# Retention and a bilinear FFN on one core: how the first pairs of slots keep their state and form their outputs

## The chip, the cores and the metric

The kernel runs on one core of one Trainium2 chip. The metric is the time of one execution in device microseconds, as the median of several runs. Beside it stands one profiled execution, from which every view of the trace comes.

## The reference

The work is a retention layer and, behind it, a feed-forward network (FFN) without a bias.

```python
batch, n_heads, seq, head_dim = (4, 8, 768, 64)
gamma = 1.0 - 2.0 ** (-5.0 - np.arange(H))
for t in range(S):
    state = gamma * state + einsum('bhd,bhe->bhde', k[:, :, t], v[:, :, t])
    y[:, :, t] = scale * einsum('bhd,bhde->bhe', q[:, :, t], state)
x = y.transpose(0, 2, 1, 3).reshape(B * S, H * D)        # 3072 x 512
out = ((x @ w_a) * (x @ w_b)) @ w_out                    # d_ff 1536
```

The inputs and the output are float32. The kernel computes with bfloat16 operands and float32 sums.

## The kernel before, in words

The 3072 rows of x are 24 *slots* of 128 rows, six to each of the four batches. The FFN works on blocks of 2 or 4 slots (`TILES`). For each block and each of 12 slices of d_ff (`ft`), `ffn_a` forms a = x w_a and ScalarE (ACT) copies it to SBUF (`asb`); `ffn_g` forms g = x w_b and VectorE (DVE) multiplies the two into `ht`; `ffn_out` multiplies by w_out. These products are L504, L516 and L544.

The decay of the state is put into k and q: both are multiplied by tables of powers of gamma (`scaled`, L212), so that the state is a plain sum of products of k and v. Inside a chunk of 128 positions, the output is the masked product of q and k, times v; what lies before the chunk comes from q times the state.

The first batch's six slots are done as three *pairs* (u = 0, 1, 2), with even positions in one slot of the pair and odd ones in the other. A pair has two chunks c = 0 and c = 1. The functions of a pair are:

- `casts2`: the scaling of k and q (L212) and the cast of v to bfloat16 (L184), each on a given engine. GpSimd (POOL) scales pair 1's k and one slot of its q; DVE scales pair 0 and the other slot of pair 1's q.
- `flip2`: transposes of scaled k or q on TensorE (PE, L395) into a bank of PSUM, and a copy to SBUF (`kT`, `qT`; L182 on ACT, L184 on DVE).
- `scores2`: 16 products of k and q (L408) for one slot of the pair, into two banks (`at`); `mask2`: two DVE products with a mask (L418), which give `aT`.
- `update2`: 16 products of k and v (L431) added to the state, which stays in one bank of PSUM (`st`). `keep_state` then copies the state to SBUF for use as an operand.
- `intra2`: 16 products of v and `aT` (L460) into the two banks `ys[u][0]` and `ys[u][1]`, one for each chunk; `inter2`: products of the state and q (L448) on top of these.
- `leave2`: the *exit*: each bank of y is copied to `xt`, the FFN's operand, on a given engine (L182 or L184).
- `warm`: products of zeros (L483), whose results nobody reads.

In the kernel before, the state of two halves of the heads (r = 0 and 1, 64 partitions each) is copied by `keep_state` as two blocks into a block-diagonal tile of 128 rows (`gbd`), with zeros elsewhere. `inter2` then has a contraction of 128 rows: 8 products for pair 0, which has no state ahead of its first chunk, and 16 for each later pair.

PSUM has eight banks: three under the tag `ff`, handed round among `flip2`, `scores2` with `ff=True` and the FFN's a, g and o; two under `at`; one each under `y0` and `y1`; one under `st`. A tile that takes over a bank waits until the last reader of the one before is done.

The order on each engine is the order in which the program is written: the helper `seq` ties each instruction to the one before it on its engine. Waits between engines follow from the tiles that instructions write and read. So the order of the calls at the end of the function is the schedule. The last of the calls that matter here are `ffn_a(0, 0, 0, W2)` and `ffn_a(0, 1, 0, W2)`, a(0,0) and a(0,1) for the first 256 columns (pair 0), then `ffn_g(0, 0, 0, W2)`, and then `ffn_a(0, 0, W2, 2 * W2)`, the same slice for the 256 columns of pair 1; in the timeline it opens a group of eight products of L504.

`fenced` and `into` are used by later batches already: a marker copy on ACT or DVE that waits for PE's last product, and a dependency by which the next products into the same banks wait for the marker ("rows change banks").

Of the kernel before, what the change touches and what calls it, by code (L numbers as in the profile page):

```python
# [9 lines left out]
F32 = mybir.dt.float32  # L10
# [6 lines left out]
PAIRS = 3  # L17
# [6 lines left out]
def kernel(  # L24
# [10 lines left out]
    nc = tc.nc  # L35
    P = 128
    B, H, S, D = q.shape
    NCH = S // P
    HP = H // 2
# [23 lines left out]
    psff = ctx.enter_context(tc.tile_pool(name="psff", bufs=3, space=bass.MemoryType.PSUM))  # L63
    psat = ctx.enter_context(tc.tile_pool(name="psat", bufs=1, space=bass.MemoryType.PSUM))
# [6 lines left out]
    def seq(bi):  # L71
        ins = bi.ins
        prev = last.get(ins.engine)
        if prev is not None:
            tc.add_manual_dep(ins, prev.name, nosync, reason="program order")
        last[ins.engine] = ins
        return bi
# [87 lines left out]
    gst = [const.tile([P, HP, D], BF16, name=f"gst{i}") for i in range(8)]  # L165
# [14 lines left out]
    def cast(engine, dst, src):  # L180
        if engine is nc.scalar:
            seq(nc.scalar.copy(dst, src))  # L182
        else:
            seq(engine.tensor_copy(dst, src))  # L184
# [12 lines left out]
    state = {}  # L197
# [16 lines left out]
    def new_nat(t):  # L214
        kqb[t] = nat.tile([P, 2, HP, 2, D], BF16, tag="kqb", name="kqb")
        kb[t], qb[t] = kqb[t][:, 0], kqb[t][:, 1]
        vb[t] = nat.tile([P, H, D], BF16, tag="vb", name="vb")
# [17 lines left out]
    def half(i):  # L235
        return slice(64 * i, 64 * i + 64)
# [53 lines left out]
    ys, begun = {}, set()  # L290
# [3 lines left out]
    fence = {}  # L294

    def fenced(eng):

        bi = seq(eng.copy(mark, bq) if eng is nc.scalar else eng.tensor_copy(mark, bq))
        tc.add_manual_dep(bi.ins, last[mybir.EngineType.PE].name, after, reason="rows change banks")
        return bi.ins  # L300

    def into(o, c, rows, bi):
        if fence.get((o, c)) is not None:
            tc.add_manual_dep(bi.ins, fence.pop((o, c)).name, after, reason="rows change banks")
# [69 lines left out]
    kT2, qT2, ats = {}, {}, {}  # L374

    def casts2(u, on):
        if 2 * u not in kqb:
            for t in (2 * u, 2 * u + 1):
                new_nat(t)
        for (i, par), eng in on.items():  # L380
            t = 2 * u + par
            if i == V:
                cast(eng, vb[t], raws["v", t])
            else:
                scaled(eng, t, i)

    def flip2(u, i, on):
        into = (kT2, qT2)[i]
        if u not in into:
            into[u] = tra.tile([P, 2, HP, P], BF16, tag="kq"[i] + "T2", name="kq"[i] + "T2", bufs=2)  # L390
        for pars, eng in on:
            tp = psff.tile([P, 2, HP, P], BF16, tag="ff", name="tp")[:, : len(pars)]
            for m, par in enumerate(pars):
                for hp in range(HP):
                    seq(nc.tensor.transpose(tp[:, m, hp, :], kqb[2 * u + par][:, i, hp, :, :], ident))  # L395
            cast(eng, into[u][:, pars[0] : pars[0] + len(pars)], tp)

    def scores2(u, par, ff=False):
        t = 2 * u + par
        if not ff:  # L400
            both = psat.tile([P, 2, HP, P], F32, tag="at", name="at")
            at = [both[:, r] for r in range(2)]
        else:
            at = [psff.tile([P, HP, P], F32, tag="ff", name=f"at{r}") for r in range(2)]
        for hp in range(HP):
            for c in range(2):
                for r in range(2):
                    seq(nc.tensor.matmul(at[r][half(c), hp, :],  # L408
                                         kT2[u][half(r), par, hp, half(c)],
                                         qT2[u][half(r), :, hp, half(c)],  # L410
                                         start=True, stop=True, skip_group_check=True))
        ats[t] = at

    def mask2(u, par):
        t = 2 * u + par
        aT[t] = tra.tile([P, 2, HP, P], BF16, tag="aT", name="aT")
        for r in range(2):
            seq(nc.vector.tensor_tensor(aT[t][:, r], ats[t][r], masks[par].to_broadcast([P, HP, P]),  # L418
                                        op=ALU.mult))

    def update2(u, c, keep=True):
        if (u, c) == (PAIRS - 1, 1):
            return
        if (u, c) == (0, 0):
            state[0] = psst.tile([P, HP, D], F32, tag="st", name="st")
        st = state[0]
        for par in range(2):
            for hp in range(HP):
                for r in range(2):
                    t = 2 * u + par  # L430
                    seq(nc.tensor.matmul(st[half(r), hp, :], kb[t][half(c), hp, r, :],  # L431
                                         vb[t][half(c), HP * r + hp, :],
                                         start=((u, c, hp, par) == (0, 0, 0, 0)),
                                         stop=(hp == HP - 1), skip_group_check=True))
        if keep:
            keep_state(c)

    def keep_state(c):
        for r in range(2):
            seq(nc.scalar.copy(gbd[1 - c][half(r), :, half(r)], state[0][half(r), :, :]))  # L440

    def inter2(u, last=False):
        for c in range(2):
            if (u, c) == (0, 0):
                continue
            for r in range(2):
                for hp in range(HP):
                    seq(nc.tensor.matmul(ys[u][c][half(hp % 2), 2 * r + hp // 2, :],  # L448
                                         gbd[c][:, hp, half(r)],
                                         qT2[u][:, :, hp, half(c)], start=False, stop=last,  # L450
                                         skip_group_check=True))

    def intra2(u, par, begin, home=(psat, "y0", "y1")):
        if begin:
            ys[u] = [home[0].tile([P, HP, P], F32, tag=home[1 + c], name="y") for c in range(2)]
        t = 2 * u + par
        for r in range(2):
            for hp in range(HP):
                for c in range(2):
                    seq(nc.tensor.matmul(ys[u][c][half(hp % 2), 2 * r + hp // 2, :],  # L460
                                         vb[t][half(c), HP * r + hp, :], aT[t][half(c), r, hp, :],
                                         start=(begin and r == 0 and hp < 2), stop=not begin,
                                         skip_group_check=True))

    def leave2(u, on):
        J, i = where[2 * u]
        if i == 0 and J not in xt:
            xt[J] = xtp.tile([P, 4, KT, P], BF16, tag="xt", name="xt")
        for c, eng in enumerate(on):
            if eng is None:  # L470
                continue
            cast(eng, xt[J][:, i + c].rearrange("p k (m par) -> p k par m", par=2),
                 ys[u][c].rearrange("p k (par m) -> p k par m", par=2))
# [6 lines left out]
    def warm(n, pool, tag, w=2 * P):  # L480
        idle = pool.tile([P, 4 * P], F32, tag=tag, name="idle")
        for _ in range(n):
            seq(nc.tensor.matmul(idle[:, :w], zero[:, :P], zero[:, :w], start=True, stop=True,  # L483
                                 skip_group_check=True))
# [71 lines left out]
    D_, G_, A_ = nc.vector, nc.gpsimd, nc.scalar  # L556
# [5 lines left out]
    casts2(1, {(V, 0): G_, (V, 1): G_})  # L562
    cast_w(0, 2)
    flip2(0, K, [((0,), A_), ((1,), A_)])
    warm(8, psat, "y1")
    flip2(0, Q, [((0,), A_)])
    warm(4, psat, "y1")
    flip2(0, Q, [((1,), D_)])
    warm(4, psat, "y1")
    scores2(0, 0, True)  # L570
    scores2(0, 1)
    casts2(1, {(Q, 1): D_})
    flip2(1, K, [((0, 1), A_)])
    flip2(1, Q, [((1,), A_), ((0,), A_)])
    mask2(0, 0)
    mask2(0, 1)
    warm(4, psat, "y1")
    update2(0, 0)
    scores2(1, 0, True)
    intra2(0, 0, True)  # L580
    intra2(0, 1, False)
    update2(0, 1)
    leave2(0, (A_, None))
    scores2(1, 1)
    mask2(1, 0)
    mask2(1, 1)
    inter2(0, True)
    leave2(0, (None, D_))
    update2(1, 0)
    intra2(1, 0, True, (psff, "ff", "ff"))  # L590
    intra2(1, 1, False)
    inter2(1, True)
    leave2(1, (A_, D_))
    W2 = 2 * P
    ffn_a(0, 0, 0, W2)
    update2(1, 1, False)
    ffn_a(0, 1, 0, W2)
    issue_loads(100)
    cast_w(1)
# [104 lines left out]
```

## Time and profile before

| What | us |
|---|---|
| Median of 3 runs | 226.34 (226.21 to 227.09) |
| The profiled execution | 226.64 |
| Its span in the trace | 224.9 |
| PE busy | 218.7 (97%) |
| DVE, ACT, POOL busy | 96.2, 96.4, 80.4 |

All times in the views are microseconds from the span's start. A row of the timeline has start, duration, engine, line, operation, output<-input, partitions x elements, and a count, with the idle time ahead of it and what ended that in brackets; a row with a count spans from the first start to the last end. PEld is PE's loading of weights. A row of the chain has start, duration, engine and line; "issue" is time in which the engine waited for nothing that the profile shows. POOLq and SPq are the queues of POOL and SP (SyncE).

### The profile page before, as it was taken

What the parts mean: (1) busy time and instruction counts of PE and PEld (TensorE: products, weight loads), DVE (VectorE), ACT (ScalarE), POOL (GpSimd) and SP (SyncE); (2) the same over time, 40 slices, a digit from 0 to 9 for tenths busy, and PEclk for the clock granted to TensorE, in tenths of its full rate; (3) what the DMA queues carried; (4) which work ended last, traced back from release to release, by engine and by line L of the source; (5) the groups of instructions that cost most, each with busy time, mean ns of one, the idle gap of its engine ahead of it and who ended that gap; (6) DMA issues with size and microseconds to landing.
All of it is one profiled execution on the core that took longest, in us unless ns stands there. A gap on an engine that the chain in (4) does not pass through costs nothing.

```text
span 224.9 us, 6284 instructions
## 1 busy us (share of the span) xinstructions
PE 218.7 (97%) x2632; PEld 133.5 (59%) x2632; DVE 96.2 (43%) x195; ACT 96.4 (43%) x207; POOL 80.4 (36%) x105
## 2 busy tenths in 40 slices
PE   8889999999999999999999999999999999999994
PEld 8768645686456866875875444554444544444443
DVE  3784347543406435562466343544243522333300
ACT  3475335433427426455457433355433354333221
POOL 5577798773556161623535053440000000000000
PEclk9999999999999999999999999999999999999999
DMA  6999999999999998978697797944100012100022
GB/s 179 347 379 382 365 289 392 305 208 211 211 265 245 281 188 191 255 185 193 143 236 146 164 243 182 210 96 143 47 0 0 3 50 93 47 3 1 0 93 95
DMA packets 96124, 39.72 MB, mean 177 GB/s; under 512 B 76000, under 2 KB 91616, under 8 KB 96096
## 3 DMA queue, kind: packets, MB, share of 16 engines
q1 hardware_dynamic: 95952, 39.20, 68.9%
q8 instruction: 20, 0.33, 0.6%
q10 hardware_dynamic: 144, 0.13, 0.2%
q14 instruction: 8, 0.07, 0.1%
HBM read 28.31 MB, written 6.29 MB: 154 GB/s over the span
## 4 chain that ended last, share of the span: by engine, by line
PE 92%; DMA 3%; SPq 1%; DVE 1%; issue 1%; ACT 1%
PE o L544 28%; PE g L516 28%; PE a L504 28%; DMA qf<-in_q_dram 3%; PE y L321 1%; PE y L333 1%; PE at L280 1%; SPq L95 1%; PE st L257 1%; PE y L448 1%; PE st L431 1%; DVE aT L418 1%; DVE kqb L212 1%; PE y L460 0%; PE at L408 0%
## 5 line engine op out<-in xcount | busy, mean ns | idle before, releaser
L519 DVE TENSOR_TENSOR ht<-g,asb 128x256 bf16<-128x256 f32 (+1 forms) x98 | 53.9, 550 | 84.9 <-PE g L516 74.7
L516 PE MATMUL g<-xt,wb_bf 128*128 128x256 bf16 (+1 forms) x400 | 77.6, 319 | 0.1
L504 PE MATMUL a<-xt,wa_bf 128*128 128x256 bf16 (+1 forms) x400 | 77.6, 319 | 0.0
L508 ACT CAST asb<-a 128x256 bf16<-128x256 f32 (+1 forms) x98 | 46.3, 473 | 71.2 <-PE a L504 71.2
L544 PE MATMUL o<-wo_bf,ht 128*128 128x512 bf16 (+2 forms) x312 | 64.4, 363 | 0.0
L504 PEld LDWEIGHTS <-wa_bf 128*128 128x128 bf16 x400 | 38.8, 98 | 23.9 <-DVE xt L184 0.4
L516 PEld LDWEIGHTS <-wb_bf 128*128 128x128 bf16 x400 | 39.1, 98 | 23.1 <-issue 0.2
L544 PEld LDWEIGHTS <-ht 128*128 128x128 bf16 x312 | 28.7, 98 | 30.6
L212 POOL TENSOR_TENSOR kqb<-kf,ktab 128x512 bf16<-128x512 f32 x22 | 22.9, 1043 | 38.4 <-DMA kf<-in_k_dram 38.0
L182 ACT COPY osb<-o 128x512 f32<-128x512 f32 (+2 forms) x25 | 14.1, 565 | 33.4 <-PE o L544 27.7
L184 POOL CAST vb<-vf 128x512 bf16<-128x512 f32 x25 | 15.0, 612 | 21.7 <-DMA vf<-in_v_dram 15.1
L212 POOL TENSOR_TENSOR kqb<-qf,qtab 128x512 bf16<-128x512 f32 x21 | 22.3, 1064 | 0.7 <-DMA qf<-in_q_dram 0.7
L182 ACT CAST gst<-sums 128x256 bf16<-128x256 f32 x33 | 13.4, 405 | 6.1 <-DVE sums L271 2.8
L271 DVE TENSOR_TENSOR sums<-st,sums 128x256 f32<-128x256 f32 x30 | 12.7, 424 | 1.6
L286 DVE TENSOR_TENSOR aT<-at,mask 128x512 bf16<-128x512 f32 x18 | 11.5, 679 | 0.0
L483 PE MATMUL idle<-zero 128*128 128x170 bf16 (+1 forms) x56 | 8.1, 321 | 1.1 <-DVE zero L126 1.1
L344 ACT CAST xt<-y 128x512 bf16<-128x512 f32 x16 | 8.5, 584 | 0.0
L418 DVE TENSOR_TENSOR aT<-at,mask 128x512 bf16<-128x512 f32 x12 | 7.5, 680 | 0.4 <-PE at L408 0.4
L483 PEld LDWEIGHTS <-zero 128*128 128x128 bf16 x56 | 6.7, 130 | 1.3 <-DVE zero L126 1.1
L184 POOL CAST wa_bf<-wsta 128x1024 bf16<-128x1024 f32 (+1 forms) x7 | 6.4, 921 | 2.4 <-DMA wsta<-in_moe_w_a_dram 2.3
L184 POOL CAST wo_bf<-wsto 128x1024 bf16<-128x1024 f32 x6 | 6.3, 1042 | 2.3 <-DMA wsto<-in_moe_w_out_dram 2.3
L184 POOL CAST wb_bf<-wstb 128x1024 bf16<-128x1024 f32 (+1 forms) x7 | 6.4, 920 | 1.8 <-DMA wstb<-in_moe_w_b_dram 1.8
(53 smaller groups left out, 87.0 us busy)
## 6 DMA issues: line engine op xcount, KB each, us to landing
out_dram<-osb SPq DMA_DIRECT2D x23, 256.0 KB, 2.6
kf<-in_k_dram SPq DMA_DIRECT2D x18, 256.0 KB, 4.0
qf<-in_q_dram SPq DMA_DIRECT2D x18, 256.0 KB, 4.0
vf<-in_v_dram SPq DMA_DIRECT2D x18, 256.0 KB, 4.5
wsta<-in_moe_w_a_dram SPq DMA_DIRECT2D x6, 512.0 KB, 7.7
wstb<-in_moe_w_b_dram SPq DMA_DIRECT2D x6, 512.0 KB, 8.1
wsto<-in_moe_w_out_dram SPq DMA_DIRECT2D x6, 512.0 KB, 8.4
kf<-in_k_dram SPq DMA_DIRECT2D x3, 512.0 KB, 5.9
```

The lines of the kernel that those rows point to most:

```text
L182: seq(nc.scalar.copy(dst, src))
L184: seq(engine.tensor_copy(dst, src))
L212: seq(eng.tensor_tensor(dst, src, tab, op=ALU.mult))
L271: seq(nc.vector.tensor_tensor(new, u[c][:, s], old, op=ALU.add))
L286: seq(nc.vector.tensor_tensor(aT[n][:, r].rearrange("p s h d -> p (s h) d"), at[:, r].rearrange("p s h d -> p (s h) d"), mask.to_broadcast ...
L418: seq(nc.vector.tensor_tensor(aT[t][:, r], ats[t][r], masks[par].to_broadcast([P, HP, P]), op=ALU.mult))
L483: seq(nc.tensor.matmul(idle[:, :w], zero[:, :P], zero[:, :w], start=True, stop=True, skip_group_check=True))
L504: seq(nc.tensor.matmul(a[:, b0 - c0 : b1 - c0], wa_bf[:, kt, fs], xcols(J, kt, b0, b1), start=(kt == 0 and b0 == c0), stop=(kt == KT - 1 a ...
L508: seq(nc.scalar.copy(asb, a))
L516: seq(nc.tensor.matmul(g[:, b0 - c0 : b1 - c0], wb_bf[:, kt, fs], xcols(J, kt, b0, b1), start=(kt == 0 and b0 == c0), stop=(kt == KT - 1 a ...
L519: seq(nc.vector.tensor_tensor(ht[J][:, ft, c0:c1], g, asbs.pop((J, ft, c0)), op=ALU.mult))
L544: seq(nc.tensor.matmul(o, ht[J][:, ft, i * P : (i + 1) * P], wo_bf[:, ft, c0:c1], start=(ft == 0), stop=(ft == NFT - 1)))
```

## The change

Five things change, all ahead of pair 2's work:

- `keep_state` for pairs 0 and 1 copies the state in one piece of 128x256 to a tile of its own (`gst`), in place of two blocks of 64x256 into `gbd`.
- `inter2q` takes the place of `inter2` there: products of 64 rows and 64 columns, in two groups. The first group writes with rows r into bank c = r, the second with rows r into the other bank. Between the groups stands a marker copy on ACT (`fenced`). The number of products is the same: 4 and 4 for pair 0, 8 and 8 for pair 1.
- The first two groups of zero products behind pair 0's transposes of k and q (8 and 4) have 64 columns in place of 256.
- DVE masks slot (0,0) ahead of scaling pair 1's last q, and slot (0,1) behind it.
- Banks: `scores2(1, 0)` writes under `at` and `scores2(1, 1)` under `ff` (the other way round before). Pair 1's y is one tile of two banks under `at`, in place of two tiles under `ff`.

With these, some calls move: `update2(0, 1)` stands between the two `intra2` of pair 0, `update2(1, 1)` between those of pair 1 (it stood behind a(0,0)), pair 0's second exit is on ACT in place of DVE and behind the second group, and pair 1's second group and exits stand behind a(0,0).

```diff
+            keep_state(c, u if u < PAIRS - 1 else None)
+    def keep_state(c, u=None):
+        if u is not None:
+            seq(nc.scalar.copy(gst[2 * u + c + 1], state[0]))
+            return
         for r in range(2):
             seq(nc.scalar.copy(gbd[1 - c][half(r), :, half(r)], state[0][half(r), :, :]))
+    def inter2q(u, swap):
+        for hp in range(HP):
+            for c in range(2):
+                if (u, c) == (0, 0):
+                    continue
+                r = 1 - c if swap else c
+                into(u, c, r, seq(nc.tensor.matmul(
+                    ys[u][c][half(hp % 2), 2 * r + hp // 2, :], gst[2 * u + c][half(r), hp, :],
+                    qT2[u][half(r), :, hp, half(c)], start=False, stop=swap, skip_group_check=True)))
+        if not swap:
+            fence[u, 0] = fence[u, 1] = fenced(nc.scalar)
-    def intra2(u, par, begin, home=(psat, "y0", "y1")):
-        if begin:
-            ys[u] = [home[0].tile([P, HP, P], F32, tag=home[1 + c], name="y") for c in range(2)]
+    def intra2(u, par, begin, home=None):
+        if begin and home is None:
+            ys[u] = [psat.tile([P, HP, P], F32, tag=f"y{c}", name="y") for c in range(2)]
+        elif begin:
+            both = psat.tile([P, 2, HP, P], F32, tag=home, name="y")
+            ys[u] = [both[:, c] for c in range(2)]
...
-    warm(8, psat, "y1")
+    warm(8, psat, "y1", 64)
     flip2(0, Q, [((0,), A_)])
-    warm(4, psat, "y1")
+    warm(4, psat, "y1", 64)
     flip2(0, Q, [((1,), D_)])
     warm(4, psat, "y1")
     scores2(0, 0, True)
     scores2(0, 1)
+    mask2(0, 0)
     casts2(1, {(Q, 1): D_})
+    mask2(0, 1)
     flip2(1, K, [((0, 1), A_)])
     flip2(1, Q, [((1,), A_), ((0,), A_)])
-    mask2(0, 0)
-    mask2(0, 1)
     warm(4, psat, "y1")
     update2(0, 0)
-    scores2(1, 0, True)
+    scores2(1, 0)
     intra2(0, 0, True)
+    update2(0, 1)
     intra2(0, 1, False)
-    update2(0, 1)
+    inter2q(0, False)
     leave2(0, (A_, None))
-    scores2(1, 1)
+    scores2(1, 1, True)
     mask2(1, 0)
     mask2(1, 1)
-    inter2(0, True)
-    leave2(0, (None, D_))
     update2(1, 0)
-    intra2(1, 0, True, (psff, "ff", "ff"))
+    inter2q(0, True)
+    leave2(0, (None, A_))
+    intra2(1, 0, True, "at")
+    update2(1, 1, False)
     intra2(1, 1, False)
-    inter2(1, True)
-    leave2(1, (A_, D_))
+    inter2q(1, False)
     W2 = 2 * P
     ffn_a(0, 0, 0, W2)
-    update2(1, 1, False)
+    inter2q(1, True)
+    leave2(1, (A_, D_))
     ffn_a(0, 1, 0, W2)
```

More of the change, by code (lines that the diff above doesn't have):

```diff
@@ L435, in update2 @@
         if keep:
-            keep_state(c)
-    def keep_state(c):
+            keep_state(c, u if u < PAIRS - 1 else None)
[3 more added lines that the diff above has]
+            return
         for r in range(2):
             seq(nc.scalar.copy(gbd[1 - c][half(r), :, half(r)], state[0][half(r), :, :]))
+    def inter2q(u, swap):
[9 more added lines that the diff above has]
+            fence[u, 0] = fence[u, 1] = fenced(nc.scalar)
     def inter2(u, last=False):
```

## The prediction, made before the changed kernel ran

> **What bounds the kernel now.** I read the page first: span, engines, and the chain of work that ended last.
>
> ```profile
> span 224.9 us, 6284 instructions
> PE 218.7 (97%) x2632; PEld 133.5 (59%) x2632; DVE 96.2 (43%) x195; ACT 96.4 (43%) x207; POOL 80.4 (36%) x105
> PE 92%; DMA 3%; SPq 1%; DVE 1%; issue 1%; ACT 1%
> ```
>
> TensorE (PE) is the bound. Windows second (stretch, clock column, then busy us of PE, PEld, DVE, ACT, POOL): from 20 us on PE has no idle, so a change ahead of that moves the end by what it moves the FFN's start. In 10 to 11 us PE is busy for half.
>
> ```profile
> 10.00:11.00 1.00, 0.50 (x6) 0.32 (x5) 1.00 (x2) 0.44 (x1) 1.00 (x2) 1.00 1.15 346
> 20.00:24.00 4.00, 4.00 (x39) 3.59 (x37) 1.27 (x3) 2.19 (x6) 2.79 (x4) 1.00 1.09 382
> 28.00:34.00 6.00, 6.00 (x36) 2.94 (x35) 2.73 (x5) 1.80 (x4) 5.52 (x8) 1.00 0.98 294
> 40.00:60.00 20.00, 20.00 (x244) 14.19 (x244) 10.10 (x21) 8.00 (x19) 12.62 (x14) 1.00 1.10 242
> ```
>
> Third, the chain in the first 24 us (start, us, what):
>
> ```profile
> 3.45 5.95 DMA qf<-in_q_dram
> 9.42 1.19 DVE kqb L212
> 10.62 1.21 DVE aT L418 x2
> ...
> 11.87 0.38 PE tp L395 x4
> ...
> 14.91 0.57 issue
> ...
> 19.17 0.87 PE a L504 x8
> ```
>
> Pair 1's q lands at 9.40, DVE scales it, masks two tiles, and only then has the transpose of q a bank. My yardstick is the first product of the FFN that needs pair 1: the x8 group of L504, which starts at 19.00 (row below). Behind it the order on PE, ACT and DVE is the same in both kernels.
>
> **The front: smaller zero products.** The timeline, as start, us:
>
> ```profile
> 1.12 5.28 PE L483 MATMUL idle<-zero 128*128 128x170 bf16 x36 [1.12 <-DVE zero L126]
> 6.48 1.29 DVE L212 TENSOR_TENSOR kqb<-qf,qtab 128x512 bf16<-128x512 f32 x2 [0.20 <-DMA qf<-in_q_dram]
> 6.70 1.04 PE L483 MATMUL idle<-zero 128*128 128x256 bf16 x8
> 7.57 0.39 PE L395 MATMUL tp<-ident,kqb 128*128 128x128 bf16 x4
> 8.65 0.42 DVE L184 COPY qT<-tp 128x512 bf16<-128x512 bf16 x1 [0.88 <-PE tp L395]
> 9.13 0.64 PE L408 MATMUL at<-qT,kT 64*64 64x128 bf16 x32
> ```
>
> A zero product of 256 columns costs some 0.11 ((1.04 - 0.27) / 7); one of 64 is not in the trace: between nothing and a transpose's 0.055 ((0.39 - 0.22) / 3). Even at 0.055 the 8 end at 7.14 and the 4 at 7.72, so each transpose of q starts when DVE has scaled its q: the second at 7.77 + 0.06 = 7.83. It ends at 8.22, DVE copies until 8.68, and the scores start at 8.74, 0.39 before the row's 9.13. Neither end of the unknown price changes that.
>
> **Masks around q's scaling.** DVE now masks (0,0) before it scales pair 1's last q.
>
> ```profile
> 8.03 2.04 POOL L212 TENSOR_TENSOR kqb<-kf,ktab 128x512 bf16<-128x512 f32 x2 [3.77 <-DMA kf<-in_k_dram]
> 10.03 1.49 POOL L212 TENSOR_TENSOR kqb<-qf,qtab 128x512 bf16<-128x512 f32 x1
> L212 DVE TENSOR_TENSOR kqb<-qf,qtab x3: 684/693/1194, 6.5 to 9.4; 128x512 bf16<-128x512 f32 x3
> 10.54 2.47 DVE L418 TENSOR_TENSOR aT<-at,mask 128x512 bf16<-128x512 f32 x4
> 11.27 0.38 PE L395 MATMUL tp<-ident,kqb 128*128 128x128 bf16 x4 [0.75 <-DVE aT L418]
> 10.56 1.01 ACT L182 COPY kT<-tp 128x1024 bf16<-128x1024 bf16 x1 [1.98 <-PE tp L395]
> 11.69 1.18 ACT L182 COPY qT<-tp 128x512 bf16<-128x512 bf16 x2
> 12.92 0.42 PE L408 MATMUL at<-qT,kT 64*64 64x128 bf16 x16
> ```
>
> The same scaling takes DVE 0.69 alone and 1.19 beside POOL; POOL's third takes 1.49, its others half of 2.04 and a little. The two exclude each other: DVE, asking at 9.42, ended at 10.61, 0.54 after POOL's second had (8.03 + 2.04 = 10.07), and POOL's third lost about 0.45. The masks show no such thing. So in the new order: masks from 9.22 (scores + 0.48, when the last products of the first tile are out), two of four in 2.47, until 10.49; the scaling asks at 10.4, in the middle of POOL's third, which undisturbed runs from 10.03 to 11.07; DVE ends 0.55 later, at 11.62. POOL's v casts then lose what its scaling lost before: no change there.
>
> [...]
>
> The transposes no longer wait for masks, but for this scaling: PE starts them at 11.68 instead of 11.27, both without a gap. The first is done at 12.07, ACT's two copies (1.18) run from 12.12 to 13.30, against 12.87 before. **This step loses 0.43**, and the 0.39 of the front are spent before it. Unblocked, the scaling would end at 11.10 and the copies, after kT's end at 11.57, at 12.75 to 12.78: these are the two ends.
>
> **State in one piece, two groups, exits.**
>
> ```profile
> 12.62 0.44 PE L431 MATMUL st<-vb,kqb 64*64 64x64 bf16 x16
> 13.14 0.64 PE L460 MATMUL y<-aT,vb 64*64 64x128 bf16 x32
> 13.10 0.76 ACT L440 CAST gbd<-st 64x256 bf16<-64x256 f32 x2 [0.22 <-PE st L431]
> 15.15 0.74 ACT L182 CAST xt<-y 128x512 bf16<-128x512 f32 x1
> 16.44 0.84 PE L448 MATMUL y<-qT,gbd 128*64 128x128 bf16 x16
> 17.21 0.61 PE L504 MATMUL a<-xt,wa_bf 128*128 128x256 bf16 x4
> 17.32 0.73 DVE L184 CAST xt<-y 128x512 bf16<-128x512 f32 x1 [0.77 <-PE y L448]
> 17.86 0.37 ACT L508 CAST asb<-a 128x256 bf16<-128x256 f32 x1 [0.17 <-PE a L504]
> L298 ACT COPY lgr<-bq x4: 191/191/192, 98.8 to 178.5; 128x1 f32<-128x1 f32 x4
> 19.00 1.04 PE L504 MATMUL a<-xt,wa_bf 128*128 128x256 bf16 x8
> ```
>
> On ACT three pairs of copies (0.76) become three of 128x256, at asb's 0.37: 1.17 saved. Added are two marker copies between the groups of products (0.19 each, L298's row) and pair 0's second exit, moved here from DVE (0.74): 1.12. ACT's load stays; its order decides. By hand-overs of 0.04 to 0.05, and queued in this order on ACT:
>
> - qT copies end 13.30; first state copy to 13.68. PE: scores(1,0) and intra(0,0) from 13.35, 16 products each in 0.25, then the second update (0.44) to 14.30.
> - Second state copy 14.34 to 14.71. PE meanwhile: intra(0,1) and the first group (4 products) end at 14.67. The marker waits for them, to 14.91, and behind it on ACT stand the first exit (to 15.66), the third state copy (to 16.05) and the second exit (to 16.80).
> - The FFN's first product needs that exit: 16.85 against 17.21, so here the change is 0.36 ahead. PE has by then done the third update, the masked products and pair 1's first group; the masks (from 13.83, two at 15.13, four at 16.37) end before.
> - The second marker waits for that group (out at 16.98) and ends by 17.2; asb, queued behind it, has no input before 17.50, and PE's second group comes only behind a(0,0): no cost.
> - a(0,0) ends at 17.46, asb until 17.87. Only now comes pair 1's first exit on ACT, to 18.62; pair 1's second group (8 products) is out long before. Since both halves of its y now lie in one tile (the other banks), DVE's exit of the second half waits, in the changed program, for ACT's: 18.66 to 19.39. Before, the two overlapped and DVE was done at 18.05.
> - The x8 group starts at 19.44 instead of 19.00: **0.44 late**. PE idles some 0.9 there, having finished a(0,1) and g(0,0). Behind DVE's exit its product for g(0,0) is queued, done by 19.9; g(0,1) asks for that bank at 20.3, so the wait goes no further.
>
> Costed at nothing: the inter products. Those of L448 cost 0.028 each at full height; at 64x64 between L460's 0.0135 and that. Only the first 4 lie on the path (through the marker): 0.05 to 0.11, taken as 0.05. The update moved ahead of a(0,0) (0.44) hides under ACT's second exit and the masks; uncovered it costs 0.44. scores(1,0) now needs both masks of (0,1), done at 12.87, hidden by ACT's 13.30 with 0.43 to spare. DMA, POOL and SP keep their order.
>
> **Sum.** +0.44 on the profiled 226.64 (span 224.9 and 1.74 around it) is 227.08; that execution lies 0.30 above the median of 226.34, so the forecast is 226.34 + 0.44 = 226.78, say 226.8.
>
> **Rivals.**
>
> (1) *The scaling isn't blocked by POOL* (the 1.19 was q's late landing). The ACT chain is up to 0.55 earlier, the x8 group at 18.9 to 19.1: no change, 226.3. For: the releaser named is the DMA. Against: POOL's 1.49 at the same time. 0.18.
>
> (2) *Faster: the exits of pair 1 don't follow each other.* With asb and ACT's exit at 18.62 as the last wait, the x8 group starts at 18.67, 0.33 early; with (1) too, 0.8 early: 226.0 to 225.5. Against: the wait in the program. 0.05.
>
> (3) *A gap as at 14.91* (0.57 in which PE waited for nothing shown) falls between the updates, on ACT's chain: +1.0, 227.3. The forecast has none. It decides if it falls between 13.3 and 14.7. 0.12.
>
> (4) *Slower: PE's clock falls.* The clock column reads 1.00 throughout, yet the first 36 products took 0.14 per 170 columns against 0.11 per 256 from 6.70 on: half speed for 5 us. The change takes away 12 wide products in 6.7 to 8.3 and lengthens the pause before the transposes from 0.75 to 1.15. Against: in 10 to 11 us PE is half idle and the zero products at 12.09 are still fast. If it slows at 12 to 13 us, some 5 us of FFN run at half rate, +2.5 less 0.9 of idle, with the 0.44: about +2.0, 228.4. It decides if products of 256 columns at 17 us are 0.21 apart. 0.10.
> [...]
>
> The forecast has the remaining 0.55, with its own range 226.4 to 227.3.
>
> **Numbers.** 0.5% is 1.13 us, about what a measurement of this kernel tells from no change: below 225.2 is faster, above 227.5 slower. Forecast: 0.51 same, 0.04 slower. (1): same. (2): 0.03 same, 0.02 faster. (3): 0.07 same, 0.05 slower. (4): 0.10 slower. Together 0.02, 0.79, 0.19; I move 0.02 to faster for what I have not thought of: 0.04, 0.77, 0.19. The range leaves out (4) and most of (2) and adds the spread of the runs before (226.21 to 227.09): 225.9 to 227.9.
>
> **What would show it.** Right: scores at 8.7; DVE's scaling of 1.1 to 1.2 ending near 11.6; qT copies ending near 13.3; a(0,0) about 16.9; DVE's pair 1 exit after ACT's; the x8 group near 19.4 behind a PE idle of 0.5 to 1. Wrong: a scaling of 0.69 in the middle of POOL's; exits that overlap; products of 256 columns 0.21 apart behind 12 us; or a shift at 19 us that is gone by 30 us.

## The result and the profile after

| | median us | runs |
|---|---|---|
| before | 226.36 (225.76 to 227.19) | 22 |
| after | 226.99 (226.48 to 228.12) | 22 |

The ratio is 1.0034, 95% interval 1.0023 to 1.0045: 0.77 us slower by the ratio (0.52 to 1.02), 0.63 by the medians. The profiled execution of after took 227.4, 0.76 more than that of before. The page of after, its span, its engines and its chain of work:

```profile
span 225.7 us, 6283 instructions
PE 217.9 (97%) x2632; PEld 132.4 (59%) x2632; DVE 95.6 (42%) x194; ACT 95.8 (42%) x207; POOL 80.5 (36%) x105
PE 82%; DMA 10%; SPq 5%; POOL 1%; issue 0%; ACT 0%
```

PE is still the bound, with as many products, so the front decides. But the windows of after (stretch, busy us of PE, PEld, DVE, ACT, POOL, clock, DMA share, GB/s) show what the ones of before did not:

```profile
11.00:12.00 1.00, 0.48 (x9) 0.48 (x10) 1.00 (x3) 0.46 (x2) 1.00 (x2) 1.00 1.20 376
12.00:13.00 1.00, 1.00 (x9) 0.46 (x8) 0.66 (x2) 1.00 (x2) 1.00 (x2) 0.50 1.02 361
13.00:14.00 1.00, 1.00 (x45) 1.00 (x47) 0.00 (x0) 0.40 (x2) 0.65 (x2) 0.50 1.09 377
14.00:15.00 1.00, 1.00 (x53) 1.00 (x47) 0.94 (x2) 0.24 (x1) 0.00 (x0) 0.50 1.09 384
15.00:16.00 1.00, 1.00 (x61) 0.99 (x54) 0.63 (x2) 0.73 (x3) 0.86 (x2) 0.79 1.10 387
20.00:24.00 4.00, 4.00 (x38) 3.59 (x37) 1.40 (x4) 1.96 (x5) 3.03 (x4) 1.00 1.09 385
```

Two of the same windows in before, and the four zero products that match those at 11.98 in the timeline of after below:

```profile
12.00:13.00 1.00, 1.00 (x29) 0.77 (x31) 1.00 (x2) 0.86 (x2) 1.00 (x3) 1.00 1.09 388
15.00:16.00 1.00, 0.53 (x28) 0.38 (x30) 1.00 (x3) 0.86 (x2) 0.82 (x2) 1.00 1.08 383
...
12.09 0.60 PE L483 MATMUL idle<-zero 128*128 128x256 bf16 x4
```

In after, PE ran at half its clock from 12.00 to 15.41. PE reads as fully busy there only because its products take about twice as long: the zero products at 11.98 start 0.21 apart once the clock is down, those at 12.09 in before 0.11. The timeline of after, engine by engine (start, us, engine, line):

```profile
11.52 0.63 PE L395 MATMUL tp<-ident,kqb 128*128 128x128 bf16 x8 [1.15 <-DVE kqb L212]
11.98 1.03 PE L502 MATMUL idle<-zero 128*128 128x256 bf16 x4
17.40 0.61 PE L523 MATMUL a<-xt,wa_bf 128*128 128x256 bf16 x4
19.88 1.03 PE L523 MATMUL a<-xt,wa_bf 128*128 128x256 bf16 x8 [0.65 <-DVE xt L184]
...
9.87 1.05 POOL L212 TENSOR_TENSOR kqb<-qf,qtab 128x512 bf16<-128x512 f32 x1
10.27 1.20 DVE L212 TENSOR_TENSOR kqb<-qf,qtab 128x512 bf16<-128x512 f32 x1
19.09 0.73 DVE L184 CAST xt<-y 128x512 bf16<-128x512 f32 x1 [2.09 <-ACT xt L182]
...
11.96 1.07 ACT L182 COPY qT<-tp 128x512 bf16<-128x512 bf16 x2 [0.54 <-PE tp L395]
13.61 0.37 ACT L440 CAST gst<-st 128x256 bf16<-128x256 f32 x1 [0.58 <-PE st L431]
15.50 0.73 ACT L182 CAST xt<-y 128x512 bf16<-128x512 f32 x1
16.10 0.36 ACT L440 CAST gst<-st 128x256 bf16<-128x256 f32 x1
18.32 0.74 ACT L182 CAST xt<-y 128x512 bf16<-128x512 f32 x1
```

Three things are to be seen. DVE's scaling ends 0.55 after POOL's third (11.47 against 10.92). DVE's exit at 19.09 waits for ACT's, and the x8 group for it. And the four zero products take 1.03 where before they took 0.60. The x8 group starts at 19.88, 0.88 late; the FFN keeps these 0.88 until 85 us, 0.52 of it is left at 90 us (the 0.36 are lost by before, which stands at 84.8 us; see "The blocks of instructions") and 0.47 at PE's last product, and the span is 0.75 longer.

k's landing wanders from execution to execution (POOL's first scaling of pair 1 starts at 8.03 in before, 7.87 in after, 8.47 in e8_keep_before), so below the x8 group is also given from that start ("from k"): 10.97 in before, 12.01 in after.

### The profile page after: what moved, and what is told of

Same layout as the page of the kernel before. It is cut to its first block, busy times and chain, and to the rows that moved or that the text cites. A ratio compares the mean times of both kernels' runs of the same rounds, so it can differ in the third digit from the quotient of the medians.

```text
span 225.7 us, 6283 instructions
## 1 busy us (share of the span) xinstructions
PE 217.9 (97%) x2632; PEld 132.4 (59%) x2632; DVE 95.6 (42%) x194; ACT 95.8 (42%) x207; POOL 80.5 (36%) x105
## 4 chain that ended last, share of the span: by engine, by line
PE 82%; DMA 10%; SPq 5%; POOL 1%; issue 0%; ACT 0%
PE o L563 28%; PE a L523 24%; PE g L535 24%; DMA wstb<-in_moe_w_b_dram 4%; DMA kf<-in_k_dram 4%; SPq L95 3%; DMA wsto<-in_moe_w_out_dram 3%; PE y L321 1%; SPq L103 1%; PE at L280 1%; PE y L333 1%; PE st L257 1%; POOL kqb L212 0%; POOL wo_bf L184 0%; POOL wb_bf L184 0%
## 5 line engine op out<-in xcount | busy, mean ns | idle before, releaser
L502 PE MATMUL idle<-zero 128*128 128x170 bf16 (+2 forms) x56 | 7.1, 299 | 1.1 <-DVE zero L126 1.1
L502 PEld LDWEIGHTS <-zero 128*128 128x128 bf16 x56 | 5.9, 127 | 1.3 <-DVE zero L126 1.1
```

## The experiments

"x8" is the start of the x8 group in the profiled execution, "quiet" the longest stretch there between 7 and 18 us in which PE has no product but transposes. Every timed run carries its mean granted clock; 3.41 us at half rate in a span of 225 take 0.0076 off it, and the runs at 0.989 to 0.992 stand clearly apart from those at 0.997 to 1.000. The last columns count them; before's 82 runs are those taken beside the experiments, since the 22 above have no clock on record. In a run that wasn't profiled, where its dip lay is not recorded.

| kernel | ratio to before (95%) | x8, from k | quiet | runs with a dip | median with, without |
|---|---|---|---|---|---|
| before | | 19.00, 10.97 | 2.31 | 0 of 82 | –, 226.29 |
| after | 1.0034 (1.0023–1.0045) | 19.88, 12.01 | 2.74 | 5 of 22 | 227.84, 226.84 |
| e1_wide | 1.0042 (1.0023–1.0060) | 20.40, 12.52 | 2.50 | 3 of 11 | 228.14, 226.82 |
| e2_order | 1.0034 (1.0017–1.0052) | 18.92, 10.95 | 2.70 | 3 of 10 | 227.74, 227.13 |
| e3_tiles | 1.0025 (1.0006–1.0043) | 19.13, 11.25 | 2.79 | 3 of 12 | 227.57, 226.77 |
| e4_narrow_before | 1.0000 (0.9986–1.0013) | 18.49, 10.56 | 2.70 | 2 of 12 | 227.11, 226.06 |
| e5_keep_after | 1.0054 (1.0036–1.0072) | 19.09, 11.05 | 1.15 | 0 of 6 | –, 227.45 |
| e6_keep_order_tiles | 1.0049 (1.0027–1.0070) | 18.19, 10.19 | 1.09 | 0 of 12 | –, 227.04 |
| e7_keep_order | 1.0057 (1.0035–1.0079) | 18.82, 10.95 | 1.00 | 0 of 6 | –, 227.42 |
| e8_keep_before | 1.0041 (1.0019–1.0062) | 19.04, 10.57 | 0.80 | 0 of 9 | –, 226.97 |
| e9_order_tiles | 1.0016 (1.0002–1.0031) | 18.99, 10.98 | 2.85 | 2 of 12 | 227.51, 226.46 |
| e10_order_tiles_24 | 1.0022 (1.0009–1.0035) | 18.10, 10.09 | 2.71 | 3 of 12 | 227.26, 226.54 |
| e11_keep_before_28 | 0.9995 (0.9983–1.0007) | 18.77, 10.55 | 0.78 | 0 of 12 | –, 226.11 |
| e12_keep_after_28 | 1.0030 (1.0018–1.0041) | 18.96, 11.03 | 1.06 | 0 of 7 | –, 226.91 |

### The zero products' width

**e1_wide**: after, with the first zero products at full width again.

```diff
-    warm(8, psat, "y1", 64)
+    warm(8, psat, "y1")
-    warm(4, psat, "y1", 64)
+    warm(4, psat, "y1")
```

> The changed kernel with the first 12 zero products at 256 columns again. Theory A (two waits: DVE's scaling blocked by POOL, pair 1's exits one after the other): they stay, the scores begin near 9.0 but the scaling still ends near 11.6 behind POOL's third; the x8 group near 19.4; 0.4 us (0.2%) over the kernel before; the clock column stays 1.00. Theory B (the time is lost to the clock that fell to 0.50 behind 12 us, for want of zero products): within 0.1 us of the kernel before.

By the ratio it is 0.95 over before's (0.52 to 1.36), more than the 0.4 expected, and the clock fell all the same. Windows of e1_wide:

```profile
13.00:14.00 1.00, 0.87 (x34) 0.74 (x36) 0.22 (x1) 0.92 (x3) 0.92 (x3) 0.83 1.09 381
15.00:16.00 1.00, 1.00 (x56) 1.00 (x47) 0.61 (x2) 0.57 (x3) 0.00 (x0) 0.50 1.10 387
```

The dip lasts from 13.65 to 17.07, again 3.41 us. Wide zero products don't prevent it in the changed order.

**e4_narrow_before**: before, with the same two groups at 64 columns (the opposite edit).

> The kernel before with 64 columns in the 8 and the 4 zero products. Theory A: the scores begin 0.4 earlier, but pair 1's q still lands at 9.4, so nothing moves behind 9.4: within 0.15 us of the kernel before. Theory B: the clock column falls to 0.50 near 12 us, and the time is 0.4 to 0.6 us over the kernel before.

Nothing gained, as expected. Its timeline:

```profile
14.40 0.41 PE L448 MATMUL y<-qT,gbd 128*64 128x128 bf16 x8
15.08 0.38 PE L431 MATMUL st<-vb,kqb 64*64 64x64 bf16 x12 [0.26 <-ACT gbd L440]
18.49 1.04 PE L504 MATMUL a<-xt,wa_bf 128*128 128x256 bf16 x8
```

Two things were not expected. The eight products of L448 run through, where in the profiled execution of before PE stood 0.57 before the eighth: from k the x8 group starts 0.41 earlier. And two of its twelve runs have a dip (226.70 and 227.51), against none of 82 of before. So the narrow products are enough to let the clock fall now and then, and so (e1_wide) is the rest of the change.

### The order of the scaling

**e2_order**: after, with q's scaling ahead of both masks, as before.

```diff
-    mask2(0, 0)
     casts2(1, {(Q, 1): D_})
+    mask2(0, 0)
     mask2(0, 1)
```

> The changed kernel with pair 1's last scaling ahead of both masks again. Theory A: the scaling ends near 10.6, the second mask near 11.8, the qT copies near 12.9 (13.0 to 13.3 in the changed kernel), the x8 group near 19.0 at full clock, within 0.15 us of the kernel before. Theory B: the clock falls as before and the time stays 0.6 us over the kernel before.

The x8 group came as expected and no time was won. Its timeline:

```profile
9.39 1.17 DVE L212 TENSOR_TENSOR kqb<-qf,qtab 128x512 bf16<-128x512 f32 x1 [0.76 <-DMA qf<-in_q_dram]
10.48 2.47 DVE L418 TENSOR_TENSOR aT<-at,mask 128x512 bf16<-128x512 f32 x4
11.63 1.18 ACT L182 COPY qT<-tp 128x512 bf16<-128x512 bf16 x2
13.10 0.42 PE L408 MATMUL at<-qT,kT 64*64 64x128 bf16 x16
18.92 1.03 PE L523 MATMUL a<-xt,wa_bf 128*128 128x256 bf16 x8 [0.65 <-DVE xt L184]
```

The qT copies end at 12.81, but the scores of pair 1 start at 13.10, behind the end of the masks (12.95) whose tile they take over. Against after at full clock (e12_keep_after_28: qT copies until 13.08, scores at 13.13) the copies are, from k, 0.31 earlier, the scores 0.07 and the x8 group 0.08. So POOL blocks the scaling (1.20 in after, for 0.69 alone in before), but another wait stands right behind it. Why its median without a dip (7 runs) lies 0.29 above after's was not settled.

### One tile or two

**e3_tiles**: after, with the two banks under `at` as two tiles of one bank each (in the other places that use them too).

```diff
-            both = psat.tile([P, 2, HP, P], F32, tag=home, name="y")
-            ys[u] = [both[:, c] for c in range(2)]
+            ys[u] = [psat.tile([P, HP, P], F32, tag=f"{home}{c}", name="y") for c in range(2)]
```

> The changed kernel with the two banks under the tag at as two tiles everywhere, so that pair 1's two exits need not follow each other. Theory A: DVE's exit runs beside ACT's, the x8 group near 18.7 at full clock (up to 0.4 later where the clock falls): 0.3 us under the kernel before at full clock, at most 0.1 over it on the median. Theory B: 0.6 us over the kernel before.

Its timeline, in which the clock fell at 12.00 as in after:

```profile
18.33 0.74 ACT L182 CAST xt<-y 128x512 bf16<-128x512 f32 x1
18.34 0.73 DVE L184 CAST xt<-y 128x512 bf16<-128x512 f32 x1 [1.33 <-PE y L450]
19.13 1.05 PE L520 MATMUL a<-xt,wa_bf 128*128 128x256 bf16 x8
```

The exits run side by side, and from k the x8 group is 0.76 earlier than in after: shown, this wait costs 0.76 at the FFN's start. Of it little reaches the end: at most 0.1 over before's was expected on the median, and 0.52 was measured. Against before, the lead of every kernel with split tiles shrinks (or its lag grows) by 0.23 to 0.26 between 111 and 115 us, and the end of its span lies 3.44 to 3.74 behind PE's last product, against 3.42 in after and 3.14 in before. In the median without a dip 0.07 is left here. The first loss stands at one multiply of DVE into `ht`, at 112.3 to 113.4: all four kernels with split tiles have 0.81 to 0.83 of idle ahead of it, where before and after have 0.45 ahead of each multiply near it, and PE's next product of a waits for it. Why DVE is late there, and what is lost at the end, was not settled.

**e9_order_tiles**: both edits, of e2_order and e3_tiles.

> The changed kernel without both waits (scaling ahead of the masks, two tiles under at) and without any added zero products. Theory A with fetching (an engine stands when the next block of its instructions comes late): the pause is short enough for the clock, x8 group at 18.1 to 18.3, a gap of at most 0.4 us near 100 us; 0.2 to 0.6 us under the kernel before.

The exits overlap (both from 18.20), but the clock, expected to hold, fell from 12.87 to 16.28, which puts the x8 group back to where before has it. Without a dip the median is 226.46, 0.38 under after's and still 0.16 over before's, where 0.2 to 0.6 under was expected.

### Keeping the clock

**e5_keep_after**: after, with eight more wide zero products between the transposes of pair 1's k and q.

```diff
     flip2(1, K, [((0, 1), A_)])
+    warm(8, psat, "y1")
     flip2(1, Q, [((1,), A_), ((0,), A_)])
```

> The changed kernel with 8 more zero products of 256 columns in the pause of TensorE between the transposes of pair 1's k and q (0.9 us of work in 1.4 us of pause), so that no window of 3.4 us is quiet there. Theory A (two waits cost 0.4 us in every execution; the clock falls in some executions and adds 0.4 to 1): clock 1.00, x8 group at 19.3 to 19.5, 0.3 to 0.5 us over the kernel before. Theory B (the clock is all of it): within 0.15 us of the kernel before.

The 3.4 us there is the length of the dips in after and e1_wide (3.41 each); that the clock goes by stretches of that length is an estimate from them, and no run shows it. The clock stayed at 1.00. This is the changed program as it was forecast; its timeline:

```profile
10.04 1.04 POOL L212 TENSOR_TENSOR kqb<-qf,qtab 128x512 bf16<-128x512 f32 x1
10.26 1.38 DVE L212 TENSOR_TENSOR kqb<-qf,qtab 128x512 bf16<-128x512 f32 x1
12.13 1.07 ACT L182 COPY qT<-tp 128x512 bf16<-128x512 bf16 x2 [0.54 <-PE tp L395]
16.61 0.61 PE L523 MATMUL a<-xt,wa_bf 128*128 128x256 bf16 x4
17.52 0.75 ACT L182 CAST xt<-y 128x512 bf16<-128x512 f32 x1
18.30 0.73 DVE L184 CAST xt<-y 128x512 bf16<-128x512 f32 x1 [2.10 <-ACT xt L182]
19.09 1.03 PE L523 MATMUL a<-xt,wa_bf 128*128 128x256 bf16 x8 [0.65 <-DVE xt L184]
```

The x8 group is 0.96 earlier than after's from k, so the dip's price there is 0.96. Yet the time is 1.2 over before's, for 0.3 to 0.5 expected, instead of less than after's.

**e7_keep_order** and **e6_keep_order_tiles**: the same line in e2_order, and in e9_order_tiles.

> The run with the scaling ahead of the masks, which was 0.3% over the kernel before though its profiled execution had the x8 group at 18.9, now with the 8 zero products in the pause. Theory A: the clock fell in its timed executions and not in the profiled one; now 1.00, x8 group at 18.9 to 19.0 and within 0.15 us of the kernel before. Rival C (something behind the x8 group costs it 0.7): still 0.5 to 0.9 us over the kernel before.

> The changed kernel without both waits (scaling ahead of the masks; the banks under at as two tiles) and with the 8 zero products in the pause. Theory A: qT copies end near 12.9, exits overlap, clock 1.00, x8 group at 18.1 to 18.3, 0.6 to 0.9 us under the kernel before. Theory B: within 0.15 us of the kernel before.

Both had the x8 group where it was expected (18.82 and 18.19) at full clock, and both were slower than before by over 1 us by the ratio. In e6_keep_order_tiles the FFN starts 0.8 ahead of before's.

**e8_keep_before**: the same line in before.

> The kernel before with the 8 zero products in the same pause. Theory A: its pause is short enough for the clock in nearly all executions; within 0.15 us of the kernel before, x8 group at 18.9 to 19.1. Theory B says the same; if it is over 0.3 us faster, the kernel before loses to the clock as well.

It is slower by 0.93 by the ratio, so it is not the change that loses here. Two rows of its timeline show the place:

```profile
99.70 1.24 PE L544 MATMUL o<-wo_bf,ht 128*128 128x512 bf16 x5 [0.16 <-issue]
101.86 1.45 PE L544 MATMUL o<-wo_bf,ht 128*128 128x512 bf16 x6 [0.92 <-issue]
```

The output products of L544 stop behind the fifth and PE stands for 0.92, waiting for nothing that the profile shows. e5, e6 and e7 have the same stop, and go on at 100.6 to 101.5 (0.46, 0.39 and 0.71). In that stretch of e8_keep_before one 16 KB packet of the instruction queue that, by its count, serves PE (20 packets for some 5,260 instructions) is under way, from 99.1 to 100.5.

### The blocks of instructions

Eight products are 16 PE instructions, a load and a product each (the page counts 2632 of both). If the stop is the edge of a block of instructions that is fetched too late, giving the 16 back ahead of it must remove it.

**e11_keep_before_28** and **e12_keep_after_28**: e8_keep_before and e5_keep_after with 28 longer zero products at the start in place of 36, for the same work.

```diff
-    warm(36, psat, "y1", 170)
+    warm(28, psat, "y1", 219)
```

> The kernel before with the 8 zero products in the pause (0.4% slower) and 28 leading zero products of 219 columns in place of 36 of 170, so that TensorE's instruction count behind them is that of the kernel before. Fetching: the gap of 1.3 us near 100 us is gone, within 0.2 us of the kernel before. Rival (the added products themselves cost it): still 0.6 to 1 us over.

> The changed kernel with the 8 zero products in the pause and 28 leading ones of 219 columns: clock held and TensorE's count as in the changed kernel. Fetching: no gap near 100 us, clock 1.00, x8 group near 19.1; 0.2 to 0.5 us over the kernel before (DVE's late last DRAIN, 0.28, among them), where with 36 leading ones it was 1.2. Rival: still 1 to 1.4 us over.

The same place in the timeline of e11_keep_before_28:

```profile
99.47 3.83 PE L544 MATMUL o<-wo_bf,ht 128*128 128x512 bf16 x17 [0.16 <-issue]
```

Seventeen products without a stop, and the ratio goes from 1.0041 to 0.9995; e12_keep_after_28 goes from 1.0054 to 1.0030. That the number of instructions ahead decides is shown. In time, e11 came as expected, and e12 with 0.68 a little over its 0.2 to 0.5. In e12 a shorter stop (0.36) appears at 119.9.

That the reason is a late block is borne out by where the stops lie. Counted in PE's loads and products ahead of each, before's gap at 14.91 lies at 447, a pause of 0.27 in before at 84.8 at 2238, the stops of e5 to e8 at 2750 and that of e12 at 3262. They are 1791, 512 and 512 apart, which are 7, 2 and 2 times 256 but for one instruction. And at each of them PE goes on 1.35 to 1.54 behind the landing of a packet of that queue. In e11 the same place in the count, 2750, comes 2.4 behind the packet's landing, and PE doesn't stop.

**e10_order_tiles_24**: e9_order_tiles with 24 zero products of 255 columns at the start.

> The same with 24 leading zero products of 255 columns in place of 36 of 170: as long, with 24 instructions less, so that each edge of a block of TensorE's instructions falls 12 products later in the code. Fetching: x8 group as in the run with 36, gaps behind 80 us differ, the one near 100 us is gone; 0.5 to 0.8 us under the kernel before. Without fetching: the same time as with 36.

The x8 group came 0.9 ahead of before's and the stop near 100 us was not there, both as expected. The time was not: the profiled execution was 0.32 faster than before's, the median 0.45 slower, 0.24 without the dips that three of twelve runs had. Between 111 and 115 us it lost the 0.24 told above, at the end of the span 0.30 more. What the timed runs lose beyond that is open.

## Why the prediction was right

226.8 was forecast and 226.99 measured, within the range and on the "same" side of 0.5%. The steps, against e5_keep_after, which has the clock that was assumed:

- **Scores early**: 8.59 there and 8.60 in after, for 8.74. Worth nothing in e4_narrow_before, as said.
- **The blocked scaling**: right. It ends at 11.64 there, 0.56 behind POOL's third, for 11.62. "POOL's v casts then lose what its scaling lost before" holds too: the four span 2.77 in after, 2.28 in e2_order. But "this step loses 0.43" was attributed to the wrong place: with the old order 0.08 comes back, since pair 1's scores need both masks. The wait that was costed at nothing "with 0.43 to spare" is the next in line.
- **ACT's chain**: in the right order, each copy too late. The first two state copies were forecast until 13.68 and 14.71, came until 13.53 and 14.55; a(0,0) at 16.61 for 16.85. Copies whose input is ready start some 0.1 before the one ahead has ended: in after by 0.13 (exit 15.50 to 16.23, state copy from 16.10) and by 0.10 (that copy to 16.46, the second exit from 16.36). At the x8 group, behind all these copies, the forecast is 0.35 too late (19.44 for 19.09).
- **Exits in turn**: right. DVE's exit waits for ACT's, 18.30 for 18.66. Rival (2) did not happen; its price of 0.77 did (0.76 in e3_tiles). Nor did rival (3): PE has no such gap between 13.3 and 14.7 in after or in e5.
- **The x8 group**: 0.44 late was forecast. From k it stands at 11.03 to 11.05 in the two kernels with the changed order at full clock, and at 10.55 to 10.57 in the three of the old order whose profile lacks the 0.57 gap: **0.48**. That it is so near 0.44 is luck, since two errors cancel: ACT's overlaps, and the gap of before's profiled execution (0.41), which was taken as part of before. PE goes on there 1.5 behind the landing of a packet of its instruction queue, as near 100 us (1.4); how many timed runs have the gap was not measured.
- **Rival (4), the clock**: it was right in kind, in 5 of 22 runs, and too dear. The "some 5 us of FFN" at half rate are one stretch of 3.41, and of the "about +2.0" the clock's part (1.6) is 1.0 (227.84 against 226.84). Its cause, fewer products and a longer pause around the transposes, fits the table: with 2.31 us or less without other products no run of 134 dipped, with 2.50 or more 21 of 91. What decides within a program was not shown. In after the dip begins 6.83, twice its own 3.41, behind the clock's rise at 5.17. That the clock goes by a grid of such stretches from its rise on is an estimate from this distance; by it the stretch ahead of e1_wide's dip holds 2.29 of the quiet one, and one of before holds all of its 2.31 without a dip. PE's idle time alone, with transposes counted as work, orders the stretches of that grid in the profiles without such an overlap: 1.51 to 1.62 in the four ahead of a dip, at most 1.21 in any other between the clock's rise and 16 us. So the longer pauses may be the cause without the transposes; no run here separates the two, and what share of a stretch decides stays open.
- **Not in the sum: the end**. The span of after ends 3.42 behind PE's last product, of before 3.14. Every kernel with the change and unsplit tiles has 3.42 or 3.43, with a dip or without. In the records DVE's closing instruction comes 0.39 to 0.41 behind SP's there, 0.03 in before. DVE runs another number of instructions there (194 in after for 195 in before); that the edge of a block of them falls to the end is only argued. The four kernels of the old order have 3.12 to 3.27, so a part of the 0.28 may wander.

So 0.48 of waits and 0.28 at the end make 0.76, and e12_keep_after_28, which has both, no dip and no stop near 100 us, measured 0.68 (0.41 to 0.93). Against e11_keep_before_28, which has the same zero products in the old order and ran beside it, it is 0.80 slower by the medians; the stop at 119.9 in e12's profile, if the timed runs have it, is part of that. Against the 82 runs of before the runs of after without a dip are 0.55 slower (0.48 against the 22 beside them), and the dips in a quarter of them put the median 0.15 higher. That this is less than 0.76 may come from before's timed runs standing at the edges of blocks as its profile does: e4 without a dip and e11, whose profiles have neither of before's two stops, are 0.23 and 0.19 under it.

The dips lasted 3.41 each: 12.00 to 15.41 in after, 13.65 to 17.07 in e1_wide, 12.87 to 16.28 in e9_order_tiles. The longest pause of PE in the quiet stretch was 1.15 in after and 1.49 in e1_wide. Whether transposes hold the clock as other products do was not shown: the table fits if they don't, but so do the pauses alone, as said. The prediction had the fewer products and the longer pause in rival (4), at 0.10, which was too little for a dip in 5 of 22 runs.

## What to carry to other kernels

Here two engines that copied out of two banks of one tile went one after the other (0.76 at the next stage), so give each bank its own tile where both are read at once, and look for what the split moves elsewhere. A stretch of pauses and transposes can cost the clock though the longest pause in it is 1.15 us (after) or 1.49 (e1_wide): eight products in it kept the clock in all 31 runs of the changed order that had them. Price a dip at its measured length (3.41 us here), not as the rest of the stage. A kernel that waits for nothing shown (0.92 in e8_keep_before) may stand at the edge of an instruction block; compare kernels whose count of instructions ahead of the dense part is the same, or a few added products cost more than what they test (0.93 us for eight here).

## What was unexpected of the hardware

- Eight added zero products, hidden themselves, made before 0.93 us slower, by a stop 80 us later. Giving the instruction count back took 1.04 off by the ratio there (1.0041 to 0.9995) and 0.54 off in the changed kernel (1.0054 to 1.0030). The stops, before's two among them, lie 1791, 512 and 512 of PE's loads and products apart: 7, 2 and 2 times 256, less one in the first.
- With a change at the front the end of the program lies 0.28 later behind PE's last product.
- Neighbouring copies on ACT overlap when the second's input is ready, in after by 0.13 and 0.10.
- The clock fell for 3.41 us in after and in e1_wide and came back, though PE's pauses ahead of it were at most 1.15 and 1.49 us.
